# One engine order searched offline for a window attention and gated scan kernel: operations as a graph, q and k by half batches, masks on three engines

## Chip, cores and metric

The kernel runs on one core of a Trainium2 chip. The metric is the device time of one execution in microseconds (us). Times quoted are medians of several executions; a profile is one execution, and its span is about 2 us shorter than the time that is measured for it. The five engines are PE (matmul; its weight loads are listed as PEld), VectorE (DVE), ScalarE (ACT), GpSimd (POOL) and SyncE (SP), whose queue issues DMA transfers here. In both kernels PE's products go to tiles in PSUM, of which they use eight banks (the new kernel's pool is one tile of 128 x 8 x 512 fp32), and another engine copies them out from there, which is called an eviction (596 ns on average for a final product on ScalarE in the kernel before).

## The reference

Attention with a window of 32 positions to each side, over 8 batches, 8 heads, 576 positions and 64 features, then a gated block with a linear scan over the positions:

```python
def _attn_ref(q, k, v):                       # 8, 8, 576, 64 each
    scores = np.matmul(q, k.transpose(0, 1, 3, 2)) / np.sqrt(D)
    mask = np.abs(pos[:, None] - pos[None, :]) <= 32
    ...                                       # softmax over the masked scores
    return np.matmul(attn, v)

def _moe_ref(x, w_in, A_log, w_out):          # x: 8, 576, 512
    proj = x @ w_in                           # 512 x 1024
    val, gate = proj[..., :512], proj[..., 512:]
    a = np.exp(A_log)[None, None, :]
    for t in range(S):
        h = a[0, 0] * h + val[:, t, :]        # the scan
        ys[:, t, :] = h
    silu = gate * (1.0 / (1.0 + np.exp(-gate)))
    return silu * ys @ w_out                  # 512 x 512
```

## The kernel before

The 4608 tokens (8 x 576) are cut into 9 chunks of 512. A loop of software-pipelined steps handles, in each step, one pair of heads of one chunk for the attention, and one of four column blocks of an older chunk for the gated block. Each engine runs what the loop body gives it, in the order of the body: in b_start, a kernel with the same body, VectorE stood still for 15.6 us in its order until w_in had come. These are the parts that the change touches.

Loads: q and k in runs of two tokens (512 B), and a second copy of v, shifted by 64 tokens, made by DMA from one on-chip tile to another:

```python
nc.sync.dma_start(out=t.rearrange("p h c e -> p (h c) e"),
    in_=src[b, 2*hp:2*hp + 2].rearrange("h (c p j) d -> p (h c) (j d)", p=96, j=2))
...
def shift_v(b):
    E, O = vEs[b % 3], vOs[b % 3]
    nc.sync.dma_start(out=O[0:64, :], in_=E[64:128, 0:4])
    nc.sync.dma_start(out=O[64:128, :], in_=E[0:64, 1:5])
```

The decay table of the scan, built on POOL from a small vector whose load is queued behind others:

```python
def prep_a():
    nc.scalar.activation(a1, a_log, AF.Exp, bias=0.0, scale=1.0)
    nc.gpsimd.memset(arep, 1.0)
    for cc in range(4):
        nc.gpsimd.tensor_scalar(out=arep[:, cc, :], in0=arep[:, cc, :],
                                scalar1=a1[:, cc:cc + 1], scalar2=None, op0=ALU.mult)
```

The loop body, in its order (PSUM tiles `sc`, `pv`, `tr`, `pjv`, `pjg`, `fo` have one buffer each):

```python
for t in range(-3, NS + 10):
    ...                                    # loads
    fe = ch(t - 10)                        # evict a final product (ACT), store it
    a = ch(t);   sc = scores(*a)           # PE
    xs = ch(t - 2)                         # evict transposed x (DVE)
    fs = ch(t - 6)                         # silu * scan (POOL)
    live[("pr",) + a] = exp_op(*a, sc)     # ACT
    pj = ch(t - 5); pv_ = proj(pj[0], pj[1], "pjv")
    ...                                    # evict q; transpose and evict k
    mask_op(*a, live[("pr",) + a])         # DVE: probabilities times 0 or 1
    p = ch(t - 1)
    pv = pv_mm(...); norm(*p, pv)          # PE, DVE
    pg = proj(pj[0], 4 + pj[1], "pjg")     # PE; tanh on ACT, scan and silu on DVE
    ...                                    # transpose q; transpose x
    fi = ch(t - 9); final(*fi)             # PE
    ...                                    # casts of q, k (POOL) and v (ACT), shift_v
```

The softmax here doesn't subtract the row's maximum and nothing guards it: scores larger than these inputs give would overflow.

Of the kernel before, what the change touches and what calls it, by code (L numbers as in the profile page):

```python
# [10 lines left out]
ALU = mybir.AluOpType  # L11


@with_exitstack
def kernel(
# [11 lines left out]
    B, H, S, D = q.shape  # L27
    HP = H // 2
    NBLK = S // 64
    NCH = B * S // 512  # L30
    out_flat = out.rearrange("b s d -> (b s) d")

# [4 lines left out]
    def T(shape, dt, tag, bufs=1):  # L37
        return perm.tile(shape, dt, tag=tag, name=tag, bufs=bufs)

    stage = {}  # L40

    def load_qk(b, hp):
        for n, src in (("q", q), ("k", k)):
            t = T([96, 2, 3, 128], f32, n + "32", bufs=4)
            nc.sync.dma_start(  # L45
                out=t.rearrange("p h c e -> p (h c) e"),
                in_=src[b, 2 * hp:2 * hp + 2].rearrange(
                    "h (c p j) d -> p (h c) (j d)", p=96, j=2))
            stage[n, b, hp] = t

    def load_v(b, es):
        t = v32s[b % 2]
        for e in es:
            lo = 128 * e - 32
            p0, p1 = max(0, -lo), min(128, S - lo)
            nc.sync.dma_start(out=t[p0:p1, e],  # L56
                              in_=v[b, :, lo + p0:lo + p1, :].rearrange("h p d -> p h d"))

    v32s = [T([128, 5, H, D], f32, f"v32_{i}") for i in range(2)]
    for tl in v32s:  # L60
        nc.vector.memset(tl[0:32, 0], 0.0)
        nc.vector.memset(tl[96:128, 4], 0.0)
    load_qk(0, 0)
    load_v(0, (0, 1, 2, 3, 4))
    load_qk(0, 1)
    load_qk(0, 2)
    load_qk(0, 3)

    ident = T([128, 128], f16, "ident")
    masks.make_identity(nc, ident)  # L70

    mask = T([128, 16, 64], f16, "mask")
    nc.gpsimd.memset(mask, 1.0)
    nc.gpsimd.affine_select(out=mask, in_=mask, compare_op=ALU.is_ge, fill=0.0,
                            base=0, channel_multiplier=1, pattern=[[0, 16], [-1, 64]])
    nc.gpsimd.affine_select(out=mask, in_=mask, compare_op=ALU.is_ge, fill=0.0,
                            base=64, channel_multiplier=-1, pattern=[[0, 16], [1, 64]])
    nc.gpsimd.memset(mask[96:128, 7, :], 0.0)
    nc.gpsimd.memset(mask[0:32, 8, :], 0.0)

    qTs = [[T([128, 2, 288], f16, f"qT{hp}_{i}") for i in range(2)] for hp in range(HP)]
    kTs = [[T([128, 640], f16, f"kT{hp}_{i}") for i in range(2)] for hp in range(HP)]
    vEs = [T([128, 5, H, 65], f16, f"vE{i}") for i in range(3)]
    vOs = [T([128, 4, H, 65], f16, f"vO{i}") for i in range(3)]
    for tl in vEs:
        nc.vector.memset(tl[:, :, :, 64:65], 1.0)
    for row in kTs:
        for tl in row:
            nc.vector.memset(tl[:, 0:32], 0.0)
            nc.vector.memset(tl[:, 608:640], 0.0)  # L90

    a_log = T([128, 4], f32, "a_log")
    w_in16 = T([128, 4, 1024], f16, "w_in16")
    w_out16 = T([128, 4, 512], f16, "w_out16")
    w_in32 = T([128, 4, 1024], f32, "w_in32")
    w_out32 = T([128, 4, 512], f32, "w_out32")
    arep = T([128, 4, 1024], f32, "arep")

    def load_w():
        nc.sync.dma_start(out=a_log, in_=moe_A_log.rearrange("(a p) -> p a", p=128))  # L100
        nc.sync.dma_start(out=w_in32, in_=moe_w_in.rearrange("(a p) c -> p a c", p=128))
        nc.sync.dma_start(out=w_out32, in_=moe_w_out.rearrange("(a p) c -> p a c", p=128))

    def prep_w(i):
        nc.vector.tensor_copy(w_in16[:, i, :], w_in32[:, i, :])
        if i == 3:
            nc.vector.tensor_scalar(out=w_out16, in0=w_out32, scalar1=0.5, scalar2=None,
                                    op0=ALU.mult)

    def prep_a():  # L110
        a1 = T([128, 4], f32, "a1")
        nc.scalar.activation(a1, a_log, AF.Exp, bias=0.0, scale=1.0)  # L112
        nc.gpsimd.memset(arep, 1.0)
        for cc in range(4):
            nc.gpsimd.tensor_scalar(out=arep[:, cc, :], in0=arep[:, cc, :],  # L115
                                    scalar1=a1[:, cc:cc + 1], scalar2=None, op0=ALU.mult)
        nc.gpsimd.memset(arep[:, :, 512:513], 0.0)

    def cast_qk(b, hp, n, eng):
        s = stage[n, b, hp]  # L120
        d = T([96, 6, 2, 64], f16, n + "16", bufs=3)
        stage[n + "16", b, hp] = d
        eng.tensor_scalar(  # L123
            out=d.rearrange("p cj h d -> p h cj d"),
            in0=s.rearrange("p h c (j d) -> p h (c j) d", j=2),
            scalar1=1.0, scalar2=1.0, op0=ALU.mult, op1=ALU.mult)

    def cast_v(b, e):
        nc.scalar.activation(vEs[b % 3][:, e, :, 0:64], v32s[b % 2][:, e], AF.Copy,
                             bias=0.0, scale=1.0)  # L130

    def shift_v(b):
        E, O = vEs[b % 3], vOs[b % 3]
        nc.sync.dma_start(out=O[0:64, :], in_=E[64:128, 0:4])
        nc.sync.dma_start(out=O[64:128, :], in_=E[0:64, 1:5])

    def trans(b, hp, n):
        s = stage[n + "16", b, hp]
        tr = ps.tile([128, 2, 3, 96], f16, tag="tr", name="tr", bufs=1)
        for c in range(3):  # L140
            for j in range(2):
                nc.tensor.transpose(out=tr[:, j, c, :], in_=s[:, 2 * c + j], identity=ident[0:96, 0:96])  # L142
        return tr

    def evac_q(b, hp, tr):
        nc.vector.tensor_copy(qTs[hp][b % 2].rearrange("p j m -> p (j m)"),
                              tr.rearrange("p j c m -> p (j c m)"))

    def evac_k(b, hp, tr):
        nc.scalar.activation(kTs[hp][b % 2][:, 32:608].rearrange("p (m j) -> p j m", j=2),  # L150
                             tr.rearrange("p j c m -> p j (c m)"), AF.Copy, bias=0.0, scale=1.0)

    def blocks(c):
        for r in range(8):
            g = 8 * c + r
            yield r, g // NBLK, g % NBLK

    def scores(c, hp):
        sc = ps.tile([128, 2, 512], f32, tag="sc", name="sc", bufs=1)
        for r, b, i in blocks(c):  # L160
            for h in range(2):
                nc.tensor.matmul(  # L162
                    out=sc[:, h, 64 * r:64 * r + 64],
                    lhsT=kTs[hp][b % 2][64 * h:64 * h + 64, 64 * i:64 * i + 128],
                    rhs=qTs[hp][b % 2][64 * h:64 * h + 64, :, 32 * i:32 * i + 32],
                    start=True, stop=True)
        return sc

    def exp_op(c, hp, sc):
        pr = T([128, 2, 512], f16, "probs", bufs=3)  # L170
        nc.scalar.activation(pr.rearrange("p h (r m j) -> p (h r) m j", m=32, j=2),  # L171
                             sc.rearrange("p h (r j m) -> p (h r) m j", m=32, j=2),
                             AF.Exp, bias=0.0, scale=1.0 / 8.0)
        return pr

    def mask_op(c, hp, pr):
        m = mask[:, 8 - c:16 - c, :].rearrange("p r q -> p (r q)")
        nc.vector.tensor_tensor(out=pr, in0=pr, in1=m[:, None, :].to_broadcast([128, 2, 512]),  # L178
                                op=ALU.mult)

    def pv_mm(c, hp, pr):
        pv = ps.tile([128, 2, 512], f32, tag="pv", name="pv", bufs=1)
        for h in range(2):
            for r, b, i in blocks(c):
                vt = (vOs if i % 2 else vEs)[b % 3][:, i // 2, 2 * hp + h, :]
                p0 = 64 * (r % 2)
                nc.tensor.matmul(  # L187
                    out=pv[p0:p0 + 64, h, 65 * (r // 2):65 * (r // 2) + 65],
                    lhsT=pr[:, h, 64 * r:64 * r + 64], rhs=vt, start=True, stop=True)
        return pv  # L190

    def norm(c, hp, pv):
        view = pv[:, :, 0:260].rearrange("p h (r x) -> p r h x", x=65)
        rc = T([128, 4, 2], f32, "rc", bufs=2)
        nc.vector.reciprocal(rc, view[:, :, :, 64])  # L195
        x = T([128, 4, 2, 64], f16, "x16", bufs=2)
        nc.vector.tensor_tensor(out=x, in0=view[:, :, :, 0:64],
                                in1=rc[:, :, :, None].to_broadcast([128, 4, 2, 64]), op=ALU.mult)
        return pv, x
# [11 lines left out]
    def xevac(c, hp, pv):  # L211
        if hp == 0:
            xT[c] = T([128, HP, 512], f16, "xT", bufs=2)
# [167 lines left out]
```

## Time and profile before

Median 233.61 us (231.76 to 234.82, 4 runs in the rounds with the new kernel).

| | before |
|---|---|
| span of the profile | 231.0 us |
| first projection of PE starts | 57.9 us |
| PE busy before it / after it | 17.0 of 57.9 us / 152.7 of 173.1 us |
| last product of PE ends | 227.4 us |

The page of the profile. The rows of digits cut the span into 40 equal slices (5.8 us each) and give the busy share in tenths; PEclk is the clock granted to PE. The last line is the chain of waits, shared out by engine.

```profile
span 231.0 us, 5289 instructions
...
PE 169.7 (73%) x2112; PEld 92.6 (40%) x2112; DVE 163.0 (71%) x284; ACT 124.4 (54%) x182; POOL 117.7 (51%) x109
...
PE   0141025274988699989989949997999988989952
...
DMA  7999999699999999999999899999561121121323
...
DMA packets 83464, 45.49 MB, mean 197 GB/s; under 512 B 39920, under 2 KB 76784, under 8 KB 83440
...
PE 42%; DVE 15%; DMA 13%; ACT 9%; SPq 8%; POOL 6%; issue 3%; POOLq 1%; ACTq 0%; DVEq 0%
```

PE is nearly idle in most of the first ten slices, then mostly at 8 or 9 tenths, and DMA is at 9 tenths in 25 of the first 28 slices, until about 160 us. PE leads the chain, but with 42% only: VectorE, DMA, ScalarE and others share it. Pieces of the chain are the load of the decay vector and its table on POOL, and then the copies of v by DMA:

```profile
25.31 5.08 DMA a_log<-in_moe_A_log_dram
30.81 12.29 POOL arep L115 x4
...
72.90 6.12 DMA vO_122<-vE_119
...
112.24 4.13 DMA vO_121<-vE_118
...
132.49 4.95 DMA vO_122<-vE_119
...
153.29 4.93 DMA vO_120<-vE_117
```

The chain in order of time, one step (start, length, what):

```profile
187.59 0.37 ACT osb L261
...
188.08 1.03 ACT probs L171
...
189.13 0.69 DVE probs L178
...
189.98 0.70 DVE x_3155 L197
...
190.72 0.40 PE pv L205 x4
191.12 0.88 PE fo L255 x4
```

Six operations on three engines, plus short gaps, close a loop: the eviction of a final product precedes exp on ScalarE, exp feeds the mask, the normalised x follows it on VectorE, its transposes precede the next final product on PE, and that releases the next eviction. One step takes 4.43 us (final products at 186.69 and 191.12), and there are 36 steps.

### The profile page before, as it was taken

Reading aid. Unit: us, or ns where it says so; the run is one execution under the profiler, and the core shown is the slowest. Engines: PE = TensorE matmul, PEld = TensorE weight load, DVE = VectorE, ACT = ScalarE, POOL = GpSimd, SP = SyncE. Lnnn points to the kernel's source line nnn. Section 1 sums busy time; section 2 is a strip of 40 time slices with the busy share of each in tenths; the row PEclk is TensorE's granted clock in tenths of the full one; section 3 lists DMA queues with packets and bytes.
Section 4 is the critical chain, followed back from the end, with each engine's and each line's share of the span. In section 5 each row is a group of like instructions: output and inputs, shape, how many; then the busy total and the mean of one; then the engine's idle time right before and its main releaser. Section 6 shows DMA issues by size and latency. Waiting matters only on the chain.

```text
span 231.0 us, 5289 instructions
## 1 busy us (share of the span) xinstructions
PE 169.7 (73%) x2112; PEld 92.6 (40%) x2112; DVE 163.0 (71%) x284; ACT 124.4 (54%) x182; POOL 117.7 (51%) x109
## 2 busy tenths in 40 slices
PE   0141025274988699989989949997999988989952
PEld 0031013253555355545545525554555434444410
DVE  5640046287699798899889946997899788788710
ACT  0720062344656577877867836786776544533432
POOL 8400069991088557765757554565772422323420
PEclk9999999999999999999999997999999999999999
DMA  7999999699999999999999899999561121121323
GB/s 162 220 243 223 223 369 309 128 238 220 233 229 203 235 227 259 255 288 252 236 276 257 197 261 270 251 250 264 171 143 52 59 77 48 45 94 67 116 91 136
DMA packets 83464, 45.49 MB, mean 197 GB/s; under 512 B 39920, under 2 KB 76784, under 8 KB 83440
## 3 DMA queue, kind: packets, MB, share of 16 engines
q1 hardware_dynamic: 83440, 45.17, 86.7%
q8 instruction: 16, 0.26, 0.5%
q14 instruction: 8, 0.07, 0.1%
HBM read 31.46 MB, written 9.44 MB: 177 GB/s over the span
## 4 chain that ended last, share of the span: by engine, by line
PE 42%; DVE 15%; DMA 13%; ACT 9%; SPq 8%; POOL 6%; issue 3%; POOLq 1%; ACTq 0%; DVEq 0%
PE fo L255 11%; PE pjg L220 8%; PE pjv L220 8%; POOL arep L115 5%; PE tr L142 5%; SPq L56 5%; DMA vO_122<-vE_119 5%; ACT probs L171 5%; DVE probs L178 4%; PE pv L187 4%; PE pv L205 4%; ACT osb L261 3%; PE sc L162 3%; SPq L45 2%; DMA k_80<-in_k_dram 2%
## 5 line engine op out<-in xcount | busy, mean ns | idle before, releaser
L178 DVE TENSOR_TENSOR probs<-probs,mask 128x1024 f16<-128x1024 f16 x36 | 30.0, 833 | 32.1 <-ACT probs L171 32.1
L255 PE MATMUL fo<-w_out_144,fu 128*128 128x512 f16 x144 | 38.0, 386 | 3.2 <-ACT osb L261 2.9
L236 ACT ACTIVATE th<-pjg 128x512 f16<-128x512 f32 x36 | 21.5, 597 | 34.3 <-PE pjg L220 31.6
L171 ACT ACTIVATE probs<-sc 128x1024 f16<-128x1024 f32 x36 | 36.7, 1019 | 6.2 <-PE sc L162 6.2
L220 PE MATMUL pjv<-xT,w_in_143 128*128 128x512 f16 x144 | 38.4, 388 | 1.7 <-DVE h_724 L229 0.4
L220 PE MATMUL pjg<-xT,w_in_143 128*128 128x512 f16 x144 | 37.4, 382 | 0.1
L220 PEld LDWEIGHTS <-w_in_143 128*128 128x128 f16 x288 | 23.4, 98 | 24.6 <-issue 3.2
L261 ACT ACTIVATE osb<-fo 128x512 f32<-128x512 f32 x36 | 21.5, 596 | 21.8 <-PE fo L255 21.8
L241 DVE SCALAR_TENSOR_TENSOR silu<-th,pjg 128x512 f16<-128x512 f16 x36 | 23.9, 664 | 1.8 <-ACT th L236 1.8
L115 POOL TENSOR_SCALAR arep<-arep,a_213 128x1024 f32<-128x1024 f32 x4 | 12.3, 3086 | 22.3 <-ACT a_213 L112 22.3
L255 PEld LDWEIGHTS <-fu 128*128 128x128 f16 x144 | 13.0, 99 | 14.9 <-issue 4.6
L187 PEld LDWEIGHTS <-probs 128*64 128x64 f16 x576 | 13.1, 116 | 12.7 <-DMA vO_122<-vE_119 4.7
L214 DVE COPY xT<-pv 128x512 f16<-128x512 f16 x36 | 15.0, 417 | 0.8 <-PE pv L205 0.7
L195 DVE RECIPROCAL rc<-pv 128x8 f32<-128x8 f32 x36 | 7.2, 200 | 11.3 <-PE pv L187 11.3
L142 PE MATMUL tr<-ident,q_211 96*128 96x96 f16 x6 | 0.6, 273 | 14.2 <-ACT kT_0_113 L150 14.2
L187 PE MATMUL pv<-vE_117,probs 128*64 128x65 f16 x120 | 10.3, 212 | 0.0
L187 PE MATMUL pv<-vE_118,probs 128*64 128x65 f16 x120 | 9.6, 199 | 0.0
L187 PE MATMUL pv<-vO_120,probs 128*64 128x65 f16 x96 | 8.6, 215 | 1.3 <-DMA vO_120<-vE_117 1.3
L187 PE MATMUL pv<-vO_122,probs 128*64 128x65 f16 x64 | 6.1, 199 | 4.5 <-DMA vO_122<-vE_119 4.5
L187 PE MATMUL pv<-vO_121,probs 128*64 128x65 f16 x96 | 7.8, 199 | 0.9 <-DMA vO_121<-vE_118 0.9
L112 ACT ACTIVATE a_213<-a_log 128x4 f32<-128x4 f32 x1 | 0.2, 205 | 14.2 <-DMA a_log<-in_moe_A_log_dram 14.2
L142 PE MATMUL tr<-ident,k_148 96*128 96x96 f16 x6 | 0.7, 278 | 9.0 <-DVE k_148 L123 9.0
(448 smaller groups left out, 379.1 us busy)
## 6 DMA issues: line engine op xcount, KB each, us to landing
out_dram<-osb SPq DMA_DIRECT2D x36, 256.0 KB, 3.0
v_0_63<-in_v_dram SPq DMA_DIRECT2D x12, 256.0 KB, 5.6
v_1_64<-in_v_dram SPq DMA_DIRECT2D x12, 256.0 KB, 6.7
w_in_145<-in_moe_w_in_dram SPq DMA_DIRECT2D x1, 2048.0 KB, 8.1
vO_120<-vE_117 SPq DMA_DIRECT2D x6, 260.0 KB, 5.1
vO_121<-vE_118 SPq DMA_DIRECT2D x6, 260.0 KB, 3.9
v_0_63<-in_v_dram SPq DMA_DIRECT2D x8, 192.0 KB, 5.3
v_1_64<-in_v_dram SPq DMA_DIRECT2D x8, 192.0 KB, 7.1
```

The costliest lines, as they stand in the source:

```text
L56: nc.sync.dma_start(out=t[p0:p1, e], in_=v[b, :, lo + p0:lo + p1, :].rearrange("h p d -> p h d"))
L115: nc.gpsimd.tensor_scalar(out=arep[:, cc, :], in0=arep[:, cc, :], scalar1=a1[:, cc:cc + 1], scalar2=None, op0=ALU.mult)
L142: nc.tensor.transpose(out=tr[:, j, c, :], in_=s[:, 2 * c + j], identity=ident[0:96, 0:96])
L171: nc.scalar.activation(pr.rearrange("p h (r m j) -> p (h r) m j", m=32, j=2), sc.rearrange("p h (r j m) -> p (h r) m j", m=32, j=2), AF.Ex ...
L178: nc.vector.tensor_tensor(out=pr, in0=pr, in1=m[:, None, :].to_broadcast([128, 2, 512]), op=ALU.mult)
L187: nc.tensor.matmul(out=pv[p0:p0 + 64, h, 65 * (r // 2):65 * (r // 2) + 65], lhsT=pr[:, h, 64 * r:64 * r + 64], rhs=vt, start=True, stop=True)
L214: nc.vector.tensor_copy(xT[c][:, hp, :].rearrange("p (a t) -> p a t", a=2), pv[:, :, 260:388].bitcast(f16))
L220: nc.tensor.matmul(out=pj, lhsT=w_in16[:, fc, 128 * oc:128 * oc + 128], rhs=xT[c][:, fc, :], start=(fc == 0), stop=(fc == 3))
L236: nc.scalar.activation(th, pj, AF.Tanh, bias=0.0, scale=0.5)
L241: nc.vector.scalar_tensor_tensor(out=si, in0=th, scalar=1.0, in1=pj, op0=ALU.add, op1=ALU.mult)
L255: nc.tensor.matmul(out=fo, lhsT=fu[c][:, cc, 128 * tt:128 * tt + 128], rhs=w_out16[:, cc, :], start=(cc == 0), stop=(cc == 3))
L261: nc.scalar.activation(o, fo, AF.Copy, bias=0.0, scale=1.0)
```

## The change

Its intent: every operation becomes a node of a graph with dependencies and buffer slots, and each engine gets a fixed order, found offline by a search that delays operations at random, and written into the kernel as a string per engine. A planner in the kernel walks the strings with a table of durations to assign buffers; PSUM is one pool of eight banks. Besides:

- q and k come by half batches, in runs of 9 tokens (2304 B);
- the shifted copy of v is made by VectorE or ScalarE, not by DMA;
- 11 of the 36 masks are done by PE (a matmul adds -30000 before exp), 16 by VectorE, 9 by POOL;
- casts and evictions are spread over ScalarE, VectorE and POOL;
- the decay vector is loaded second, its table is four broadcast copies, weights come in twelve pieces;
- chunks 0, 1 and 8 are projected in half chunks.

```diff
-    for t in range(-3, NS + 10):
-        ... (the loop body above)
+SEQ = {
+    "pe": "mQmQKSKKmSPSQPSmtmPSPSVtVGQGKGmSGPPmVStVPPGVKtGVVQGVSSFFFKGQFFQFmm..."   # 241 letters
+    "act": "qexExhxexwhwwxwwxgegEgxhvxTgkTEgwgegqxooxEgovooeoxxETxxEoeogxg...",
+    ... (dve, pool, sp)
+}
+SHARED = {
+    "mask": "pppGppppDDppDDGppDDDDGDGGDDGGDDGGDDD",
+    "evk": "DADAAAAAAAAAAAAA",
+    ... (which engine, for each kind that may be on several)
+}
@@ masks on PE, before the scores accumulate on top
+        elif kd == "mask" and e == "pe":
+            for h in range(2):
+                half = slice(64 * h, 64 * h + 64)
+                nc.tensor.matmul(out=bf("sc", *key)[:, h, :], lhsT=madd[half],
+                                 rhs=eye8[half].rearrange("p r q -> p (r q)"), start=True, stop=False)
@@ q, k by half batches of tokens
-                in_=src[b, 2*hp:2*hp + 2].rearrange("h (c p j) d -> p (h c) (j d)", p=96, j=2))
+                in_=src[b].rearrange("(s y) (T p j) d -> T p s y (j d)", y=2, p=32, j=9)[T])
@@ the shifted copy of v
-        nc.sync.dma_start(out=O[0:64, :], in_=E[64:128, 0:4])
+            copy(e, dst.rearrange("p e h d -> p (e h d)"), src.rearrange("p e h d -> p (e h d)"))
@@ decay table
-            nc.gpsimd.tensor_scalar(out=arep[:, cc, :], in0=arep[:, cc, :], ...)
+            eng.tensor_copy(arep[:, cc, :], a1[:, cc:cc + 1].to_broadcast([128, 1024]))
```

## The prediction

> **What bounds the kernel now** (busy time by stage, timeline, chain of waits).
> (1) Start, 0 to 60 us: PE is busy 19 of 60 us; the first projection runs near 58 us. DMA is saturated. The chain goes through loads, a POOL wait of 22.3 us for the small decay vector, queued behind other loads, then 12.3 us of POOL building the decay table, with q, k casts waiting behind it.
> (2) 60 to 205 us: a step of 4.43 us, 36 in all. In PE's timeline it is full: final 0.96, scores 0.34, value projection 1.02, k transposes 0.35, pv 0.37, gate projection 0.88, q transposes 0.31, x transposes 0.23. DMA stays saturated until 160 us; shifted copies of v put four DMA pieces of 4 to 6 us on the chain.
> (3) Tail, 219 to 231 us: product and ScalarE eviction take turns on one PSUM tile, 1.75 us each.
>
> **What the change does.**
> - DMA: q, k runs go from 512 B to 2304 B; the shifts (about 4 MB) leave the queues; v stays at 256 B. [...] the trace shows 220 to 290 GB/s with q, k, v and 369 where w_in loads. Estimate: 41 MB at 250 to 310 GB/s, 130 to 160 us, no limit after the start.
> - PE: 288 transposes instead of 384; 11 of 36 masks become PE matmuls. Estimate from the step's parts: projections and finals 108 x 0.86 = 93; scores and pv 36 x 0.71 = 26; x transposes 8; q, k transposes 288 x 0.056 = 16; masks 2.5; 85 changes of array mode at 0.1 = 8. Sum 153 us, against 36 x 4.43 = 160.
> - VectorE loses 20 masks (0.83 each) and most q evictions, gains 17 shifts: about 145 us. ScalarE about 130, POOL about 105 (estimates).
> - Start: decay vector loaded second, its table split over two engines; weights cast in pieces; chunks 0, 1, 8 in halves. Queued before the last w_in piece: 6.8 MB, at 230 to 300 GB/s 23 to 30 us, so projections start at 25 to 30 us.
> - Tail: eight PSUM banks shared freely: 5 us, not 11.
>
> **Sum.** PE does about 8 us of its work before 28 us, then 145 us with 2 to 4% of stalls, then 5 us of last eviction and store: 28 + 145 + 4 + 5 = 182. The offline order probably overlaps the start better and hides some mode changes: I predict **178 us**, range **167 to 192**; chances: faster by over 2% 0.97, within 2% 0.02, slower 0.01. The 55 us: about 30 from the start, 10 from PE work and its gaps, 9 from vanished DMA waits, 6 from the tail.
>
> **What would show it.** Right: PE at 9 tenths from 30 us to the end; a chain mostly of PE, without DMA after 40 us; under 60,000 packets; first projection before 32 us; decay table off the chain. Wrong: PE digits of 7 or 8 in the middle with waits for other engines; waits for q, k, v loads after 60 us.
>
> **What would make it wrong.** Four engines near 70 to 85% full in fixed orders leave little slack: a duration unlike the one that the order assumes delays everyone. Likeliest is POOL against VectorE: [...] here one VectorE cast took 3.66 us beside a POOL memset against 0.55 alone, the masks 0.83 on average against 0.69. More POOL work (v casts, nine masks) could stretch both. Strided q, k evictions could cost more than 1.2 us, and v at 256 B could starve the start.

The parts of PE's work: 93 + 26 + 8 + 16 + 2.5 + 8 = 153.5, for its 153 us. The estimate of 250 to 310 GB/s was from the rates in the page before: 197 to 288 GB/s in the slices from 46 to 162 us, and 369 in the slice where w_in loads. The 0.1 us for a change of array mode is in the traces. They print the shape of the array for each matmul (`128*128`, `64*128` or `128*64`); in the new kernel four matmuls of 512 columns take 0.86 us after others of the same shape (98.20 us) and 0.97 us after the scores (100.02 us), and the shape changes 85 times.

## The result, and the profile after

177.79 us median (177.44 to 178.49, 4 runs) against 233.61. The ratio is 0.7621, with a 95% interval of 0.758 to 0.7663. Ratios here are the mean time of one kernel's fast runs over that of the other's of the same rounds, so they are not quite the ratio of the medians.

| | before | after | difference |
|---|---|---|---|
| span of the profile | 231.0 | 176.1 | -54.9 |
| start of the span to first projection | 57.9 | 30.1 | -27.8 |
| first projection to end of the last product | 169.5 | 142.4 | -27.1 |
| last product to end of the span | 3.6 | 3.6 | 0 |

The page of the profile after (slices of 4.4 us):

```profile
span 176.1 us, 5221 instructions
...
PE 156.5 (89%) x2134; PEld 101.3 (58%) x2134; DVE 143.0 (81%) x233; ACT 130.8 (74%) x172; POOL 114.3 (65%) x117
...
PE   1164969989999999999999999999999999999991
...
PEclk9999985899999999999999999999999999999999
DMA  4999999789998999999999999898980311311155
...
DMA packets 53670, 41.22 MB, mean 234 GB/s; under 512 B 39312, under 2 KB 39312, under 8 KB 53648
...
PE 57%; DVE 11%; ACT 11%; POOL 6%; issue 5%; SPq 5%; DMA 3%; ACTq 0%; POOLq 0%; DVEq 0%
```

PE stands at 8 or 9 tenths from the seventh slice (26 us) to the last but one, VectorE is at 81% and ScalarE at 74%. The only DMA piece left on the chain is a load of k at 9.7 us. The busy time by stage, for both kernels, from the first projection on (the columns are PE, PEld, DVE, ACT and POOL busy, granted clock, DMA share, GB/s; the first two numbers are the stage and its length). Before:

```profile
57.90:231.00 173.10, 152.74 (x1854) 79.43 (x1852) 136.17 (x225) 106.12 (x156) 88.36 (x82) 0.99 0.80 185
```

After:

```profile
30.10:176.10 146.00, 140.70 (x1904) 90.09 (x1902) 127.65 (x197) 116.04 (x157) 96.67 (x85) 0.99 0.79 226
```

Each stage ends with 3.6 us after the last product. Without these, PE stood idle for 173.1 - 152.7 - 3.6 = 16.8 us before and 1.7 us after. So of the 54.9 us, 27.8 are the earlier first projection, 15.1 are PE's gaps, and 12.0 are PE's busy time that went away (152.7 - 140.7; before the first projection it hardly changed, 17.0 and 15.8 us). PE's busy time is rough, as its ends are modelled.

The chain in order of time in the middle of the new kernel runs along PE, one product after another, across the kinds (L469 q and k transposes, L580 final, L552 projection, L522 pv, L498 scores):

```profile
98.20 0.86 PE psum L552 x4
99.07 0.38 PE psum L522 x16
99.44 0.57 PE psum L498 x32
100.02 0.97 PE psum L552 x4
100.99 1.00 PE psum L469 x18
101.99 0.86 PE psum L552 x4
```

No loop through the other engines is left there: whatever PE does next is ready. It is not so everywhere. Between 47 and 64 us and between 72 and 90 us most of the chain runs through ScalarE, VectorE and POOL, although PE is busy 42.4 of the 43 us from 47 to 90: there PE is fed just in time.

### The profile page after: what moved, and what is told of

It reads as the page before. It is cut to its first block, busy times and chain, and to the rows that moved or that the text cites. A ratio compares the mean times of both kernels' runs of the same rounds, so it can differ in the third digit from the quotient of the medians.

```text
span 176.1 us, 5221 instructions
## 1 busy us (share of the span) xinstructions
PE 156.5 (89%) x2134; PEld 101.3 (58%) x2134; DVE 143.0 (81%) x233; ACT 130.8 (74%) x172; POOL 114.3 (65%) x117
## 2 busy tenths in 40 slices
DMA packets 53670, 41.22 MB, mean 234 GB/s; under 512 B 39312, under 2 KB 39312, under 8 KB 53648
## 4 chain that ended last, share of the span: by engine, by line
PE 57%; DVE 11%; ACT 11%; POOL 6%; issue 5%; SPq 5%; DMA 3%; ACTq 0%; POOLq 0%; DVEq 0%
PE psum L552 26%; PE psum L580 14%; PE psum L522 5%; PE psum L469 4%; PE psum L537 4%; PE psum L498 4%; DMA stg<-in_k_dram 3%; ACT pr L503 3%; SPq L448 3%; DVE f2k L560 2%; DVE si L565 2%; DVE vO L401 2%; DVE pr L512 2%; ACT f2k L398 2%; POOL fu L575 1%
## 5 line engine op out<-in xcount | busy, mean ns | idle before, releaser
L552 PE MATMUL psum<-xT,w_in 128*128 128x256 f16 (+1 forms) x384 | 70.7, 329 | 0.0
L552 PEld LDWEIGHTS <-w_in 128*128 128x128 f16 x384 | 35.8, 99 | 20.6 <-issue 0.2
L560 DVE TENSOR_TENSOR_SCAN f2k<-arep,f2k,psum 128x512 f32<-128x512 f32 (+1 forms) x44 | 44.4, 1028 | 1.9 <-PE psum L552 1.3
L503 ACT ACTIVATE pr<-psum 128x1024 f16<-128x1024 f32 x36 | 36.5, 1035 | 8.1 <-PE psum L498 7.5
L575 POOL TENSOR_TENSOR fu<-f2k,si 128x512 f16<-128x512 f32 x24 | 30.0, 1257 | 11.1 <-DVE si L565 6.8
L580 PE MATMUL psum<-w_out,fu 128*128 128x512 f16 x144 | 35.1, 379 | 0.1
L563 ACT ACTIVATE th<-psum 128x512 f16<-128x512 f32 x36 | 21.8, 605 | 8.6 <-PE psum L552 8.6
L565 DVE SCALAR_TENSOR_TENSOR si<-th,psum 128x512 f16<-128x512 f16 x36 | 24.1, 676 | 3.2 <-ACT th L563 3.1
L398 ACT ACTIVATE f2k<-psum 128x512 f32<-128x512 f32 x35 | 20.8, 611 | 6.9 <-PE psum L580 6.2
L531 DVE TENSOR_TENSOR x<-psum,rc 128x512 f16<-128x512 f32 x36 | 24.1, 683 | 0.6
L572 POOL TENSOR_TENSOR fu<-f2k,si 128x512 f16<-128x512 f32 x12 | 14.0, 1174 | 13.7 <-DVE f2k L560 6.6
L580 PEld LDWEIGHTS <-fu 128*128 128x128 f16 x144 | 13.2, 98 | 13.5 <-issue 0.2
L469 PE MATMUL psum<-ident,q 128*128 128x128 f16 x144 | 11.6, 231 | 6.4 <-ACT q L398 5.3
L398 ACT ACTIVATE kT<-psum 128x1152 f16<-128x1152 f16 x14 | 16.0, 1145 | 1.2 <-PE psum L469 1.2
L498 PEld LDWEIGHTS <-kT 64*128 64x128 f16 x576 | 11.2, 99 | 8.5 <-issue 4.8
L498 PE MATMUL psum<-qT,kT 64*128 64x64 f16 x576 | 14.5, 197 | 1.8 <-DVE kT L401 1.5
L522 PEld LDWEIGHTS <-pr 128*64 128x64 f16 x576 | 12.0, 114 | 6.9 <-issue 3.9
L522 PE MATMUL psum<-vE,pr 128*64 128x65 f16 x320 | 14.7, 201 | 0.9 <-ACT pr L503 0.3
L469 PEld LDWEIGHTS <-q 128*128 128x128 f16 x144 | 9.8, 103 | 9.5 <-ACT q L398 5.8
```

The lines of the kernel that those rows point to most:

```text
L398: nc.scalar.activation(dst, src, AF.Copy, bias=0.0, scale=mul)
L469: nc.tensor.transpose(out=t[:, 128 * j:128 * j + 128], in_=s[:, j].rearrange("p y d -> p (y d)"), identity=ident)
L498: nc.tensor.matmul(out=sc[:, h, 256 * t + 64 * r:256 * t + 64 * r + 64], lhsT=kT[64 * h:64 * h + 64, 64 * i:64 * i + 128], rhs=qT[64 * h:6 ...
L503: nc.scalar.activation(bf("pr", *key), bf("sc", *key), AF.Exp, bias=0.0, scale=1.0 / 8.0)
L522: nc.tensor.matmul(out=pv[p0:p0 + 64, h, x0:x0 + 65], lhsT=pr[:, h, at:at + 64], rhs=vt, start=True, stop=True)
L531: nc.vector.tensor_tensor(out=x, in0=view[:, :, :, 0:64], in1=bf("rc", *key)[:, :, :, None].to_broadcast([128, 2, 4, 64]), op=ALU.mult)
```

## The experiments

Names that begin with b are edits of the kernel before, names with a are edits of the new kernel. All gave correct results. The time of the kernel before, in the rounds of each group, was 232.5 to 234.9 us.

### The start alone (b_start)

```diff
+    nc.sync.dma_start(out=a_log, ...)          # now the first load of all
-        nc.gpsimd.memset(arep, 1.0)
-            nc.gpsimd.tensor_scalar(out=arep[:, cc, :], in0=arep[:, cc, :], ...)
+            nc.gpsimd.tensor_copy(arep[:, cc, :], a1[:, cc:cc + 1].to_broadcast([128, 1024]))
-        if t == -1:
-            prep_a()                           # now before the loop
```

> The kernel before, with only the decay vector loaded first and its table made by four broadcast copies at once. If the start was lost to that wait and that table (26 us of ScalarE and POOL held up between 16.5 and 43 us), the time falls from 233 to 208 to 218 us and PE's first projection comes at 38 to 46 us instead of 58. The rival: the saturated DMA queues were the real limit of the start and of the first 160 us; then the waits only move to loads and the time falls by less than 8 us.

Measured: 231.87 us, ratio 0.9931 (0.9845 to 1.0016). The first projection starts at 55.9 us, not 57.9. In the time the two kernels can't be told apart. The waits that I had named were gone, and others stood behind them. Its chain in order of time:

```profile
27.39 9.95 DMA w_in<-in_moe_w_in_dram
...
41.93 1.03 ACT probs L169
42.98 1.35 DVE probs L176
...
53.90 5.84 DMA vO<-vE
```

VectorE now waits 15.6 us for w_in, in its order, before it may evict anything; then the loop through exp, mask and normalised x; then a shifted copy of v. The rival was right about the size: waits moved to loads, and to the order. The loop body puts the first projection in its sixth step (`proj` of `ch(t - 5)`), and it starts beside the sixth exp, which begins at 57.97 us before and 55.99 us here; w_in had landed at 35.5 and 37.3 us, about 20 us earlier.

### The run length (b_runs)

```diff
-                in_=... "h (c p j) d -> p (h c) (j d)", p=96, j=2))
+                in_=... "h (p c j) d -> p h (c j d)", p=96, j=2, c=3))     # 1536 B
-        kTs[...][:, 32:608].rearrange("p (m j) -> p j m", j=2)             # step of 4 B
+        kTs[...][:, 32:608].rearrange("p (m c j) -> p j c m", c=3, j=2)    # step of 12 B
         (q: in order before, now with a step of 6 B)
```

> The kernel before, with q and k loaded in runs of 1536 B instead of 512 B, nothing else. If the run length is what limited the loads, packets fall from 83,000 to about 59,000, GB/s in the first 160 us rises above 270 and the time falls by 5 us or more. If PE's full step and the waits of the start set the pace, the DMA share falls but the time stays within 2% of 233 us. I expect the second, 228 to 233 us.

Measured: 246.37 us, ratio 1.0544 (1.0466 to 1.0623). Packets fell to 58,888 as expected, but the test was spoiled by its own side effect. The group of k evictions:

```profile
L149 ACT ACTIVATE kT<-tr 128x576 f16<-128x576 f16 x32 | 67.1, 2098 | 16.1 <-PE tr L142 14.4
```

They took 2098 ns each with writes in a step of 12 B, against 813 to 821 ns before with a step of 4 B; in b_shiftstartruns, with the same runs but writes in order, they take 651 ns. A q eviction on VectorE, now writing with a step of 6 B, took 1119 ns instead of about 446. Why the larger steps cost that much the runs don't show. So this run says nothing about run length. The new kernel writes in order and reads PSUM with a step: 1152 elements in 1145 ns on ScalarE.

### The tail (b_tail)

```diff
-        fo = ps.tile([128, 512], f32, tag="fo", name="fo", bufs=1)
+        tag = ("pjv", "pjg", "fo", "pjv")[tt] if c == NCH - 1 else "fo"
+        fo = ps.tile([128, 512], f32, tag=tag, name=tag, bufs=1)
```

> The kernel before, with the final products of the last chunk in three PSUM banks instead of one. If product and eviction taking turns in one bank cost the tail 3 to 4 us, the time is 229 to 230.5 us; if the last store and the last multiply on POOL set the end, it stays within 1 us of 233.

Measured: 228.35 us, ratio 0.9768 (0.9688 to 0.9848). In the profile, the time from the end of the last silu on VectorE to the end of the span falls from 10.5 us (220.47 to 231.0) to 8.1 us (217.34 to 225.4). That is 2.4 us of the 5.6 us between the two profiles; the rest lies before the tail, where the edit changes nothing. One difference there is the clock: 0.96 from 120 to 160 us before (recorded at half from 138.6 to 142.0 us, after a wait of 3.2 us for a copy of v), and 1.00 in b_tail. The fast runs of the kernel before spread by 3 us in these rounds, too. Turn-taking in one bank did cost the old tail; whether it was 2 or 5 us stays open.

### The three together (b_all)

The edits of b_start, b_runs and b_tail in one kernel.

> The three together: 200 to 210 us if the gains add up. What then still separates it from the new kernel's 178 us (22 to 32 us) belongs to the shifts of v on the DMA queues, to PE's shorter work and to the order of the operations.

Measured: 241.96 us, ratio 1.0337 (1.0272 to 1.0402). It carries the slow evictions of b_runs, so the sum that I expected can't be read from it.

### The shifted copies off the DMA queue (b_shift)

```diff
-        nc.sync.dma_start(out=O[0:64, :], in_=E[64:128, 0:4])
-        nc.sync.dma_start(out=O[64:128, :], in_=E[0:64, 1:5])
+        nc.vector.tensor_copy(O[0:64]..., E[64:128, 0:4]...)
+        nc.scalar.activation(O[64:128]..., E[0:64, 1:5]..., AF.Copy, bias=0.0, scale=1.0)
         (called one step later, so that the cast it needs is done)
```

> The kernel before, with only the shifted copies of v made by VectorE and ScalarE instead of DMA. In its trace PE stands still for 13.5 us between 58 and 219 us, and the DMA copies of v are the pieces of the chain there. If they are the cause, the time falls by 7 to 12 us, to 222 to 226 us. The rival: a step of 4.43 us in which VectorE is busy 90% has no room for the copies (0.8 us on VectorE, 2 us on ScalarE, once in 4.5 steps), and the time stays within 2%.

Measured: 234.00 us, ratio 1.0118 (1.0018 to 1.0219). The rival holds. The chain in order of time where a shift falls:

```profile
112.33 1.15 ACT vE L129 x2
...
113.50 1.94 ACT vO L135
...
115.95 1.03 ACT probs L172
...
117.00 0.69 DVE probs L179
```

No wait for a DMA copy of v is left, but exp stands behind the copy on ScalarE, and the loop of 4.43 us starts late by it: from the starts of the final products, a turn with a copy takes 6.67 us. Between the copies it still takes 4.43 us (final products at 79.00 and 83.44 us). In the kernel before, the long turns between the first final product and the last full step add up to 8.2 us beyond 4.43 us each, most of them beside a DMA copy of v; here the turns with copies add up to 10.2 us. So the edit did not only take waits out, it put copies in their place, and the gain that I had written down for the DMA waits isn't there in this order. Both copies on VectorE (0.70 us each), as the new kernel has 17 of its 20, were not tried in the old order.

### Both (b_shiftstart), and with longer runs (b_shiftstartruns)

The edits of b_shift and b_start together; then also runs of 1536 B, with evictions written in order:

```diff
-        kTs[...][:, 32:608].rearrange("p (m j) -> p j m", j=2)  <-  tr.rearrange("p j c m -> p j (c m)")
+        kTs[...][:, 32:608].rearrange("p (m c j) -> p m c j", c=3, j=2)  <-  tr.rearrange("p j c m -> p m c j")
```

> The same, and the decay vector first with its table made by copies. Alone the latter gave nothing clear (ratio 0.993): in its trace the next wait, a DMA copy of v at 54 to 60 us and w_in, landing at 37 us, took its place. If the waits of the start stand one behind the other, the two together give more than the sum of the two alone: 208 to 218 us. If w_in and the in-order wait of VectorE for it hold the start alone, it gives no more than b_shift.

> The same again, with q and k in runs of 1536 B, and with their evictions written in order (b_runs wrote with a step of 12 B, and a k eviction took 2.10 us instead of 0.82; that cost hid what the runs give). If the loads set the start once the other waits are gone, w_in lands some 5 us earlier and the time falls by 3 to 7 us against b_shiftstart. If not, the two are within 2 us.

Measured: 229.96 us, ratio 0.9921 (0.9852 to 0.999), and 234.47 us, ratio 1.0133 (1.0064 to 1.0203). The first projection starts at 53.5 and 51.7 us (the profile of the first is a slow run). Neither expectation held in size. The wait for the decay vector with its table, and the DMA copies of v, each visible in the trace and taken away together, leave the old order within 1% of where it was. The longer runs bring the first projection forward by 1.8 us, but VectorE is busy 174.0 us instead of 162.2, mostly with q evictions (747 ns instead of about 446, now reading PSUM with a step), and leads the chain with 37%. So this run doesn't isolate the run length either.

### The searched order alone (a_greedy)

```diff
 SEQ = {
-    "pe": "mQmQKSKKmSPSQPSmtmPSPSVtVGQGKGmSGPPmVSt...",
+    "pe": "QQKmmSSKKmSSPPQtmmSSPPVVGGtQKVGVGmmSSPPPKP...",   # from a plain rule, all five engines
 (operations, engines, load order, buffers and planner unchanged)
```

> The new kernel with the same operations, engines, tiles and buffers, but each engine's order taken from a plain rule (the operation that can start first, the oldest step first on a tie) instead of the searched order. If the searched order matters, the time is 195 to 215 us, with PE at 6 to 8 tenths in the middle and waits of PE for other engines. If the gain lies in the operations, the eight free banks and the loads, and any sensible order would do, it stays within 3% of 178 us.

Measured: 203.60 us, ratio 0.8716 (0.8661 to 0.8771). Its page:

```profile
PE 160.4 (80%) x2134; PEld 106.0 (53%) x2134; DVE 151.7 (76%) x233; ACT 133.4 (67%) x172; POOL 115.1 (57%) x117
...
PE   0085589769999679989988989898989586989752
```

The first projection starts at 29.2 us, as early as in the new kernel, and DMA is as free. What it lacks is PE's density: 122.0 us busy of 137.0 between 29 and 166 us (busy time by stage), where the new kernel has 1.6 us of gaps in 135.9. In a_greedy:

```profile
29.00:166.00 137.00, 121.95 (x1686) 79.79 (x1685) 113.49 (x166) 105.75 (x138) 86.59 (x77) 0.98 0.81 226
```

and in the new kernel:

```profile
30.10:166.00 135.90, 134.26 (x1875) 87.29 (x1874) 124.31 (x192) 112.33 (x151) 94.35 (x83) 0.99 0.81 229
```

Of the 24.2 us between the two profiles, about 19 are PE's gaps and 6 are PE's busy time, part of that at half clock (the trace has it from 41.4 to 48.2 us, after an idle gap of 2.4 us; nine transposes took 1.12 us at 43.87 us and 0.67 us at 33.17 us). The searched order is worth 203.6 - 177.8 = 26 us; the operations, banks, loads and engine choices under a plain order are worth the other 30.

### The shifts by DMA in the new kernel (a_dmashift, a_actshift)

```diff
         elif kd == "sh":
-            copy(e, dst..., src...)
+            nc.sync.dma_start(out=dst, in_=src)        # a_dmashift
+            nc.scalar.dma_start(out=dst, in_=src)      # a_actshift
```

> The new kernel with the shifted copies of v made by DMA again, as before, issued in the same place of the order. If the shifts on the DMA queue cost what I put down for them (9 us), the time is 184 to 190 us, with DMA pieces between v tiles on the chain. The rival: they relieve VectorE of 12 us of copies and the larger runs leave the queues room, so the time is the same or up to 3 us shorter.

> The new kernel with the shifts by DMA, but issued from ScalarE's queue and not behind the loads in the one queue of SP. a_dmashift cost 31 us. If that is the place in the queue (the copies wait behind loads already queued, and SP waits for a cast before it may issue the next load), most of it goes away: 178 to 188 us. If the transfers themselves are slow beside saturated loads, it stays at 200 to 212 us.

Measured: 209.11 us, ratio 0.8942 (0.8872 to 0.9011), and 212.28 us, of which only one run, 208.68 us, was fast, so there is no ratio. Waits in total, how often, longest, in a_dmashift:

```profile
PE psum L522 <- DMA vO<-vE: 24.8, 6, 11.4
```

and in a_actshift:

```profile
PE psum L522 <- DMA vO<-vE: 27.3, 7, 6.0
```

The cost is 31 us: the first projection comes at 41.0 us instead of 30.1, and PE waits 24.8 us for the copies, partly within that start. A queue of its own doesn't help. In a_dmashift SP waits 19.5 us for casts of v before it may issue copies, which holds up the loads behind them; in a_actshift that wait is gone from SP, and the time is no better. So, as far as one run can show it, the place in the one queue is not what costs most. The transfers land 4.4 us (12 large) and 6.6 us (8 small) after issue in the one, 5.4 and 5.6 us in the other, where a copy of the large size on VectorE takes 0.82 us. That an order made for 0.8 us can't hide 5 is my reading of this. Whether a new search could place DMA copies early enough was not tried.

### PE's clock at the start (a_warm)

34 matmuls without a use, into free PSUM banks, in PE's gaps before 28 us:

```diff
+WARM = {1: (14, 2), 3: (1, 6), 4: (1, 2), 6: (4, 2), 7: (2, 2), 8: (1, 2), 10: (1, 2), 12: (5, 4), ...}
+            n, at = WARM.get(len(done), (0, 0))
+            for _ in range(n):
+                nc.tensor.matmul(out=psum[:, at, :], lhsT=ident, rhs=eye8..., start=True, stop=True)
```

> The new kernel with 34 matmuls without a use, put into PE's idle gaps between 5 and 27 us. In the new kernel PE works from 25.7 to 33.9 us at a granted clock of 0.5, in matmuls of twice the length. If PE is the limit there, a clock at full rate is worth up to 4 us: 174 to 176.5 us. If loads and the other engines set the pace until 55 us, as the chain between 47 and 90 us suggests, it stays within 1 us of 178.

Measured: 175.54 us (173.59 to 176.42), ratio 0.7493 (0.7423 to 0.7564). Every run, the one slow run of 176.42 us too, is below every run of the new kernel (177.44 to 178.49). The two were timed in different rounds; the gain is 1.7% from the two ratios to the kernel before (0.7493 / 0.7621) and 1.3% from the medians. The profile is of the slow run. Busy time by stage, 26 to 34 us, in the new kernel:

```profile
26.00:34.00 8.00, 7.63 (x104) 5.83 (x102) 5.12 (x9) 5.87 (x9) 6.39 (x7) 0.60 0.95 249
```

and in a_warm:

```profile
26.00:34.00 8.00, 7.89 (x133) 6.66 (x132) 5.83 (x11) 7.25 (x11) 6.54 (x8) 1.00 1.04 242
```

PE is as busy in both, but at a clock of 0.60 it gets through 104 instructions, at 1.00 through 133, two of them without a use. The new kernel's trace has the half clock from 25.5 to 32.3 us, so not quite as long as I had written. The durations agree: eight matmuls of 256 columns on the chain took 1.82 us at 30.12 us and 0.87 us at 42.72 us. Nine transposes of q took 1.14 us at 10.45 us, before the first record of the clock (22.1 us), and 0.67 us at 95.73 us. The first projection comes at 28.4 us instead of 30.1. This is the fastest version, faster than both kernels.

### All masks on VectorE (a_dvemasks)

```diff
-    "mask": "pppGppppDDppDDGppDDDDGDGGDDGGDDGGDDD",
+    "mask": "DDDDDDDDDDDDDDDDDDDDDDDDDDDDDDDDDDDD",
     (each moved mask stands in VectorE's order where its exp ends)
```

> The new kernel with all 36 masks on VectorE, as before (11 leave PE, 9 leave POOL), each put into VectorE's order where its exp ends; every other order as it was. If spreading the masks is what keeps four engines in balance, VectorE, 143 us busy of 176 in the new kernel, gets 20 x 0.8 = 16 us more and becomes the limit: 184 to 194 us, VectorE over 85% busy. If VectorE's slack takes them, or if its contention with the POOL masks (2.2 us each) was as dear as the masks, the time stays within 3% of 178 us.

Measured: 190.77 us, ratio 0.8268 (0.814 to 0.8397). VectorE is busy 159.2 us of 187.6, 85%, and PE 82%. The time is inside the first expectation. The order was not searched again for it, so part of the 13 us can be the order; that VectorE can't take them for nothing is shown.

## Why the prediction was right or wrong

**The total** was right: 178 predicted, 177.79 measured. Most signs that it named are there too. PE is dense (8 or 9 tenths) from 26 us on, the first projection comes at 30.1 us (before 32), packets are 53,670 (under 60,000), no DMA piece lies on the chain after 16 us, the decay table is off it, and DMA falls from 8 tenths to 0 at about 132 us (130 to 160 was the estimate for all bytes, stores included).

**The sum** has one term that was clearly off. It was 28 + 145 + 4 + 5 = 182; measured are 30.1 us to the first projection, 142.4 us to the end of the last product (149 predicted for 145 + 4), and 3.6 us after it. The middle term was too large because I let PE do "about 8 us of its work" before the first projection. The trace shows 15.8 us busy in the first 30.1 us, part of it at half clock. PE's whole work was 156.5 us, not 153, and its stalls were 1.7 us, not 4. So the sum was 6 us too long for the span and left out the 2 us by which the measured time exceeds the span. I lowered 182 to 178 by a guess that the order overlaps the start better; the guess happened to be the size of what was left, so that the total came out within 0.3 us is luck.

**"About 30 from the start"** was right in size (27.8) and half right in cause. What I put first, the wait for the decay vector and the table on POOL, was not it: without both, b_start gained 0.7%, which is not clear of noise, and its first projection came 2 us earlier. The next waits stood right behind: w_in, the in-order wait of VectorE for it, and the loop body, which has five steps before the first projection. The estimate from the bytes before the last piece of w_in (23 to 30 us) did hold: that piece landed at 28.6 us in the new kernel, and the first projection followed 1.5 us later, where the old kernel let about 22 us pass. a_greedy shows that this needs the new operations, engines and loads but not the searched order: under a plain order the first projection comes at 29.2 us. The copies of v are part of it (by DMA it comes at 41.0 and 37.9 us). I did not split the rest.

**"9 from vanished DMA waits"** failed as a step that can be had alone. The waits were there (most of 8.2 us of long turns in the old kernel), and in the new one PE's gaps fell by 15.1 us. But b_shift swapped those waits for copies on VectorE and ScalarE in the old kernel and the time did not fall (1.0118). What the runs showed in their place is a loop of 4.43 us through ScalarE, VectorE and PE, which starts late by whatever is put before exp, here 2.2 us for the copies of a batch. A wait on the chain is worth its length only if nothing of the same length takes its place. In the new kernel the same copies by DMA cost 31 us. The cost of an operation belongs to the operation and the order together.

**"10 from the step's PE work and its unfilled gaps"** rested on "PE's timeline is full", and that reading was half of the truth. At 99 to 110 us it is full. But after 180 us the q and k transposes are gone, PE is busy 21.83 of 25 us, and a turn still takes 4.43 us: the loop sets it, not PE. The busy time by stage:

```profile
180.00:205.00 25.00, 21.83 (x268) 10.00 (x269) 20.56 (x34) 11.35 (x17) 6.20 (x6) 1.00 0.17 64
```

PE's work and the loop happened to have the same length. The new kernel leaves both: PE's total busy time falls by 13.2 us (169.7 to 156.5; I predicted 7), and the loop is gone from the chain. I take it that independent work stands between its members now; no run tests that alone.

**"6 from the tail"** was too large. From the end of the last VectorE operation that feeds the output to the end of the span it is 10.5 us before (silu, 220.47) and 7.3 us after (scan, 168.84): 3.2 us. PE works through seven final products in a row there, at 0.86 us each, and that sets the tail now.

**What I feared** came, and was not dear. Work that ran on POOL and VectorE at the same time took longer in several places: one cast of v on VectorE took 1.27 us, 0.99 us of it beside a multiply on POOL, and two others 0.41 us (beside a cast on POOL) and 0.43 us; two shifted copies of v on VectorE beside POOL work took 1.40 and 1.44 us instead of 0.70; and the multiplies of 512 columns on POOL took 1257 ns on average against at most 1161 before. But PE stood idle for only 1.7 us after the first projection, so the order had room for it. The 27 evictions of q and k on ScalarE took 1.14 us, under the 1.2 that I had set as the limit; the five on VectorE took 1.35 us, over it. The first projection came at the end of the 25 to 30 us that I had counted, so v in runs of 256 B did not starve the start by more than that.

Not shown: how the 30 us that the new kernel gains under a plain order divide, what half batches, longer runs and half chunks are worth alone, whether the random delays in the search made the order sturdier than a search without them, why work on POOL and VectorE took longer side by side, and what makes the clock of PE rise and fall.

## What to carry to other kernels

When several engines are each 50 to 75% busy, read the loop in the chain, turn by turn, not only the busiest engine: here the wait for the decay vector and the DMA copies of v could be taken out of the old order for a gain of under 1%, while the same operations in a searched order were 26 us faster than in a plain one. A saving on the chain may be added to a sum only if you know what is next behind it; test it by removing it alone. And after PE has become the limit, look at the clock granted to it in the first dense stretch, where 34 useless matmuls bought about 2 us.

## What the traces showed of the clock, of steps and of DMA

- PE's clock: in the new kernel the first record of it is full, at 22.1 us (nine transposes took 1.14 us at 18.90 us and 0.68 us at 23.29 us), and it fell to half at 25.5 us, although no gap of PE from 17 us on was longer than 1.2 us (PE busy 4.32 of 6.0 us from 20 to 26 us, granted clock 0.60 from 26 to 34 us). In a_warm PE was busy 5.51 of the same 6.0 us, and the clock was 1.00 from 20 to 34 us.
- The records agree with the durations from 22 us on. Before that, the page of the profile shows the full clock at 10 to 20 us, while nine transposes took 1.14 us there and 0.67 us later; the trace's first record of the clock is at 22.1 us, so that full clock is no measurement.
- The k eviction of 576 elements on ScalarE took 0.65 us written in order, 0.82 us with a step of 4 B and 2.10 us with a step of 12 B. ScalarE reading PSUM with a step of 256 B and writing in order took 1.145 us for 1152 elements, at no visible loss (exp took 1.035 us for 1024 elements in order).
- An on-chip copy of 260 KB by DMA, beside loads that kept DMA at 9 tenths in most slices, landed 4.4 us (a_dmashift, from the loads' queue) and 5.4 us (a_actshift, from a queue of its own) after issue; these are medians.
